# Attention with a gated two-layer network: ones taken out of the value tiles, softmax sums of the global queries made apart, their normalisation put a pair later, and the first batches' work reordered

## The chip, the cores and the metric

The kernel runs on one core of a Trainium2 chip. The metric is the time of one execution on the device in microseconds (us), lower is better. A run of a kernel is several such executions with other kernels in between on the same chip; where a kernel was timed in rounds, every round also ran the kernel before, so that ratios compare the same chip and the same minutes. In the profiles PE is TensorE (the matrix engine), DVE is VectorE, ACT is ScalarE, POOL is GpSimd and SP issues the DMA transfers. PSUM is the memory that TensorE writes its results to. The granted clock is the share of TensorE's full clock that the profile records; here a record is either full or half.

## The reference

Eight batches of eight heads with 512 local positions and 32 global positions of 64 numbers each. A local position attends to the 32 global keys and to local keys within 32 positions. A global query attends to all 544 keys. The 4352 rows that come out go through a network of two matrices with a gate.

```python
s_g = scale * q_g @ concat(k_g, k_l).T            # global queries: 32 x 544
out_g = softmax(s_g) @ concat(v_g, v_l)
s_ll = where(|i - j| <= 32, scale * q_l @ k_l.T, -1e9)
out_l = softmax(concat(scale * q_l @ k_g.T, s_ll)) @ concat(v_g, v_l)
x = concat(out_g, out_l)                          # per batch 544 rows of 8*64 = 512
h = x @ w_in                                      # 512 -> 2048
out = (h * clip(h + 3, 0, 6) / 6) @ w_out         # 2048 -> 512
```

## The kernel before

Work goes by pairs of heads: pair `p` is batch `p // 4`, pair `p % 4` of it (32 pairs). Pairs 0 to 7 (batches 0 and 1) are the head of the kernel, in which weights and inputs still arrive; from pair 8 on one loop body is repeated. The scheduler of the language orders each engine's queue between the pins that the kernel sets; GpSimd's and the DMA queue's order is pinned in every turn of the loop.

Three parts matter. First, the products of the global queries (`emit_PG`). Each head's value tile is 128 columns wide, 64 values and 64 ones, so the same matmul gives the weighted values in rows 0 to 63 and the softmax's sum in rows 64 to 127. All four pairs of a batch collect in one PSUM tile `pg` of a pool with a single buffer:

```python
def emit_PG(p):                                   # ten matmuls of 128x32 a pair
    if m == 0:
        pgs[b] = psg.tile([P, NM, 2, Sg], FP32, tag="pg", name="pg")   # psg: bufs=1
    for e in range(2):
        for u in range(NT):
            nc.tensor.matmul(out=pg[:, m, e], lhsT=vt[:, u, h], rhs=Eg[:, u, e], ...)
        nc.tensor.matmul(out=pg[:, m, e], lhsT=vgs[b % NV][:, h], rhs=Eg[:, NT, e], ...)
```

Second, the normalisation `emit_XG(b)`, which reads `pg` and so sets it free. The logarithm and exponential on ScalarE make the reciprocal, VectorE multiplies:

```python
def emit_XG(b):
    for e in range(2):
        nc.scalar.activation(out=Lg[e * D:(e + 1) * D], in_=pg[D:P, :, e], func=LN)
    nc.scalar.activation(out=Rg, in_=Lg, func=EXP, scale=-1.0)
    for e in range(2):
        nc.vector.tensor_tensor(out=xg[r, :, b], in0=Rg[r], in1=pg[0:D, :, e], op=mult)
```

Third, the loop. `M(n)` puts in n units of the network (four matmuls of 128x512 each, psH for the first matrix, po for the second), which is TensorE's filler:

```python
for p in range(2 * NM, NPAIR):
    feed(p)                       # loads of pair p+5, casts of pair p+4, transposes of pair p+3
    M(n[0]); emit_S2(p + 1)       # local scores, exp on ScalarE, mask multiply on VectorE
    M(n[1]); emit_SG(p + 1)       # global scores, exp on ScalarE
    M(n[2]); emit_AV(p); emit_PG(p)
    M(n[3]); emit_X(p)            # transposes of the normalised rows by DMA into xt
    if m == NM - 1:
        emit_XG(b)                # right after the batch's last products
        units += moe_units(...)
    pin(*QUEUES)
```

The softmax here doesn't subtract the row's maximum and nothing guards it: scores larger than these inputs give would overflow.

## Time and profile before

| kernel before | |
|---|---|
| median of 3 runs (lowest to highest) | 330.34 us (329.37 to 331.39) |
| span of the profiled execution, mean granted clock | 327.7 us, 0.993 |
| TensorE busy | 308.8 us, 94% |
| last w_out cast done | 55.6 us |
| first local scores of batch 2 | 75.03 us |

The table gives times after the span's start. The busy strips, TensorE's waits and GpSimd's timeline stand in the prediction. Three lines are added here, because the result turns on them. The first is the point where the loop proper begins, in TensorE's timeline of the kernel before (start, length, engine, line, operation, result and inputs, shape, count):

```profile
75.03 0.62 PE L258 MATMUL psS<-qT,kT 64*128 64x128 f16 x16
```

The second and third are the groups, by shape, of ScalarE's and VectorE's part in `emit_XG` (total busy us, then mean ns of one, then idle time of the engine in front of them):

```profile
L374 ACT ACTIVATE Lg<-pg 64x128 f32<-64x128 f32 x16 | 4.4, 274 | 3.1 <-PE pg L349 2.2
L378 DVE TENSOR_TENSOR xg<-Rg,pg 64x128 f16<-64x128 f32 x16 | 4.5, 280 | 2.5 <-ACT Rg L375 2.4
```

Per batch that is two logarithms, one exponential and two multiplies, each about 0.3 us: some 1.4 us in a row, started as soon as the batch's last products are there.

### The profile page before, as it was taken

How to read it: one execution, taken by the hardware profiler on the slowest of the kernel's cores; microseconds unless marked ns; L12 is line 12 of the kernel's file. 1: busy time of each engine (PE TensorE's matmuls, PEld its weight loads, DVE VectorE, ACT ScalarE, POOL GpSimd, SP SyncE). 2: the span in 40 equal slices, each digit the busy share in tenths (PEclk: the TensorE clock that was granted, in tenths of full speed). 3: DMA queues.
4: the chain of work that ended last, by engine and by line, in shares of the span. 5: the costliest groups of instructions: out<-in, count | busy, mean ns of one | idle time of the engine just before them, and what ended most of it. 6: DMA issues, size and time to landing. Idle time of an engine off the chain costs nothing.

```text
span 327.7 us, 7442 instructions
## 1 busy us (share of the span) xinstructions
PE 308.8 (94%) x2792; PEld 162.5 (50%) x2792; DVE 219.0 (67%) x482; ACT 196.2 (60%) x388; POOL 133.6 (41%) x226
## 2 busy tenths in 40 slices
PE   7698798979899889999999999999999999999996
PEld 3453354544455445555555555554555555448444
DVE  6677876677666759747985787579755883379201
ACT  3676673878534359546864686468655971379200
POOL 7986899165563363345544642255130000000000
PEclk9799999999999999999999999999999999999999
DMA  7999998299999999999999968898954003100122
GB/s 198 309 375 253 307 341 194 62 194 200 182 180 236 210 189 200 166 204 200 184 154 204 226 124 148 189 214 146 146 130 112 4 16 98 64 0 2 32 90 72
DMA packets 142979, 53.70 MB, mean 164 GB/s; under 512 B 130272, under 2 KB 134624, under 8 KB 142944
## 3 DMA queue, kind: packets, MB, share of 16 engines
q1 hardware_dynamic: 140768, 52.97, 75.3%
q0 software_dynamic: 2176, 0.26, 2.6%
q8 instruction: 22, 0.36, 0.5%
q14 instruction: 13, 0.11, 0.1%
HBM read 35.13 MB, written 8.91 MB: 134 GB/s over the span
## 4 chain that ended last, share of the span: by engine, by line
PE 70%; DMA 12%; DVE 6%; SPq 5%; ACT 3%; POOL 3%; issue 1%; POOLq 0%; ACTq 0%
PE po L406 31%; PE psH L390 27%; DMA qT<-qn 4%; DMA stg<-in_moe_w_in_dram 4%; PE psS L258 3%; DMA stg<-in_v_l_dram 3%; DVE gt L397 2%; ACT t L395 2%; SPq L120 2%; PE pav L324 2%; PE pav L327 2%; PE pg L347 1%; PE po L418 1%; SPq L123 1%; DVE E L265 1%
## 5 line engine op out<-in xcount | busy, mean ns | idle before, releaser
L406 PE MATMUL po<-wout,gt 128*128 128x512 f16 x528 | 121.2, 379 | 0.0
L390 PE MATMUL psH<-xt,win 128*128 128x512 f16 x512 | 119.2, 379 | 1.9 <-DMA xt<-xn 1.0
L397 DVE SCALAR_TENSOR_TENSOR gt<-t,psH 128x512 f16<-128x512 f32 (+1 forms) x144 | 91.0, 653 | 29.1 <-ACT t L395 28.5
L395 ACT ACTIVATE t<-psH,half_col 128x512 f32<-128x512 f32 (+1 forms) x144 | 91.8, 669 | 26.5 <-PE psH L390 25.8
L390 PEld LDWEIGHTS <-win 128*128 128x128 f16 x576 | 53.1, 98 | 52.9 <-issue 2.2
L406 PEld LDWEIGHTS <-gt 128*128 128x128 f16 x528 | 48.5, 98 | 53.5
L262 ACT ACTIVATE E<-psS 128x512 f16<-128x512 f32 x96 | 49.6, 604 | 39.2 <-PE psS L258 39.2
L265 DVE TENSOR_TENSOR E<-E,mk 128x512 f16<-128x512 f16 x96 | 52.0, 574 | 12.7 <-ACT E L262 11.3
L246 POOL COPY qT<-qT 128x32 f16<-128x32 f16 x24 | 5.5, 230 | 97.8 <-DMA qT<-qn 97.7
L410 ACT COPY ot<-po 128x512 f32<-128x512 f32 x16 | 9.4, 586 | 39.4 <-PE po L406 39.4
L410 DVE COPY ot<-po 128x512 f32<-128x512 f32 x17 | 11.7, 691 | 31.5 <-PE po L406 31.4
L333 DVE TENSOR_TENSOR xn<-pav,rc 128x256 f16<-128x256 f32 x64 | 26.2, 421 | 1.5
L136 POOL CAST vt<-stg 128x512 f16<-128x512 f32 x32 | 21.1, 660 | 1.2 <-DMA stg<-in_v_l_dram 1.1
L141 POOL COPY vb<-vt 64x512 f16<-64x512 f16 x32 | 20.7, 646 | 2.1
L332 DVE RECIPROCAL rc<-pav 128x4 f32<-128x4 f32 x64 | 10.3, 172 | 16.0 <-PE pav L327 15.9
L136 POOL CAST kn<-stg 128x512 f16<-128x512 f32 x31 | 19.3, 622 | 3.4 <-DMA stg<-in_k_l_dram 2.6
L136 POOL CAST qn<-stg 128x512 f16<-128x512 f32 x31 | 20.2, 650 | 0.9 <-PE psTk L222 0.5
L324 PE MATMUL pav<-vt,E 128*128 128x65 f16 x256 | 20.3, 194 | 0.0
L327 PE MATMUL pav<-vb,E 128*128 128x65 f16 x256 | 20.3, 195 | 0.0
L287 ACT ACTIVATE E<-psS 128x512 f16<-128x512 f32 x32 | 17.4, 594 | 4.8 <-PE psS L283 4.3
L324 PEld LDWEIGHTS <-E 128*128 128x128 f16 x256 | 18.0, 98 | 3.7 <-issue 0.2
L327 PEld LDWEIGHTS <-E 128*128 128x128 f16 x256 | 17.1, 98 | 3.0
(85 smaller groups left out, 266.0 us busy)
## 6 DMA issues: line engine op xcount, KB each, us to landing
stg<-in_k_l_dram SPq DMA_DIRECT2D x32, 256.0 KB, 3.5
stg<-in_q_l_dram SPq DMA_DIRECT2D x32, 256.0 KB, 4.1
stg<-in_v_l_dram SPq DMA_DIRECT2D x32, 256.0 KB, 5.0
out_dram<-ot SPq DMA_DIRECT2D x23, 256.0 KB, 2.5
stg<-in_moe_w_in_dram SPq DMA_DIRECT2D x16, 256.0 KB, 6.4
stg<-in_moe_w_out_dram SPq DMA_DIRECT2D x16, 256.0 KB, 5.2
out_dram<-ot SPq DMA_DIRECT2D x8, 192.0 KB, 2.4
out_dram<-ot SPq DMA_DIRECT2D x16, 64.0 KB, 1.9
```

What stands on the lines that cost most here:

```text
L136: eng.tensor_copy(out=o, in_=s[c + "f"])
L141: eng.tensor_copy(out=vbs[b % NV][0:D, :, hs, 0:D], in_=vts[b % NV][D:P, :, hs, 0:D])
L262: nc.scalar.activation(out=E[:, ch, e], in_=pss[2 * ch + e], func=EXP, scale=qk_scale)
L265: nc.vector.tensor_tensor(out=E[:, ch, e], in0=E[:, ch, e], in1=mk[:, ch].rearrange("p w c -> p (w c)"), op=mult)
L324: nc.tensor.matmul(out=o, lhsT=E[:, 0, e, w * P:(w + 1) * P], rhs=vt[:, w, h, 0:D + 1], start=True, stop=False, skip_group_check=True)
L327: nc.tensor.matmul(out=o, lhsT=E[:, 1, e, w * P:(w + 1) * P], rhs=vb[:, (w - 1) % NT, h, 0:D + 1], start=False, stop=True, skip_group_chec ...
L333: nc.vector.tensor_tensor(out=xn[:, 2 * w2:2 * w2 + 2].rearrange("p w (e d) -> p w e d", e=2), in0=pv[:, :, :, 0:D], in1=rc.to_broadcast([ ...
L390: nc.tensor.matmul(out=ps[:, 0:n], lhsT=w_in_t[m][:, c * P:(c + 1) * P], rhs=rhs(m), start=(m == 0), stop=(m == NM - 1), skip_group_check= ...
L395: nc.scalar.activation(out=t1[:, 0:n], in_=ps[:, 0:n], func=RELU, bias=half_col, scale=1.0 / 6.0)
L397: nc.vector.scalar_tensor_tensor(out=gts[c][:, 0:n], in0=t1[:, 0:n], scalar=1.0, in1=ps[:, 0:n], op0=amin, op1=mult)
L406: nc.tensor.matmul(out=po[t][:, 0:dm], lhsT=gts[c][:, t * P:(t + 1) * P], rhs=w_out_t[c // 4][:, c % 4], start=(c == 0), stop=(c == NC - 1))
L410: (nc.scalar.copy if t % 2 else nc.vector.tensor_copy)(out=ot, in_=po[t][:, 0:dm])
```

## The change

Its intent is to shorten TensorE's work in the loop and to fill the gaps of the head. The value tiles of two heads now lie side by side with a one at each end, so that one matmul of 128x64 serves both heads of a pair. The softmax's sums no longer come from ones in the value tile: GpSimd adds the five pieces of the exponentials (`sum_E`), and one matmul with a 128x128 tile of ones per batch (`emit_den`) sums over partitions. A reciprocal on VectorE replaces the logarithm and exponential. In the loop, `emit_den` and `emit_XG` of a batch come one pair later than before, after the local scores of the next batch's second pair. In the head, pair 2's keys and queries are loaded ahead of all values, keys and queries of batch 2 are loaded and cast in the middle of w_out, and the global scores of batch 0 move into batch 1's attention.

```diff
     def emit_PG(p):
-        for e in range(2):
-            h = 2 * m + e
-            for u in range(NT):
-                nc.tensor.matmul(out=pg[:, m, e], lhsT=vt[:, u, h], rhs=Eg[:, u, e], ...)
-            nc.tensor.matmul(out=pg[:, m, e], lhsT=vgs[b % NV][:, h], rhs=Eg[:, NT, e], ...)
+        for u in range(NT):
+            nc.tensor.matmul(out=o, lhsT=vt[:, u, m, vc], rhs=Eg[:, u] (both heads), ...)
+        nc.tensor.matmul(out=o, lhsT=vgs[b % NV][:, hs] (both heads), rhs=Eg[:, NT] (both heads), ...)
+    def sum_E(p):                                 # called at the end of emit_SG(p)
+        nc.gpsimd.tensor_tensor(out=s2, in0=Eg[:, 0:2], in1=Eg[:, 2:4], op=add)
+        nc.gpsimd.tensor_tensor(out=s2[:, 0], in0=s2[:, 0], in1=s2[:, 1], op=add)
+        nc.gpsimd.tensor_tensor(out=Ess[b][:, m], in0=s2[:, 0], in1=Eg[:, NT], op=add)
+    def emit_den(b):
+        nc.tensor.matmul(out=pgs[b][:, 1] (all pairs), lhsT=ones, rhs=Ess[b] (all pairs), ...)
     def emit_XG(b):
-        for e in range(2):
-            nc.scalar.activation(out=Lg[e * D:(e + 1) * D], in_=pg[D:P, :, e], func=LN)
-        nc.scalar.activation(out=Rg, in_=Lg, func=EXP, scale=-1.0)
         for e in range(2):
             r = slice(e * D, (e + 1) * D)
-            nc.vector.tensor_tensor(out=xg[r, :, b], in0=Rg[r], in1=pg[0:D, :, e], op=mult)
+            nc.vector.reciprocal(out=Rg[r], in_=pg[r, 1, :, e])
+            nc.vector.tensor_tensor(out=xg[r, :, b], in0=Rg[r], in1=pg[r, 0, :, e], op=mult)
     # loads, and likewise GpSimd's casts
-    for i in range(NC):
+    for i in range(8):
         load_w("out", i)
-    load(2 * NM)
+    load(2 * NM, "kq")
+    for i in range(8, NC):
+        load_w("out", i)
+    load(2 * NM, "v")
     # the head of batch 1 and 2 (cut)
+    held = [units.pop(0), units.pop(0)]           # two units kept for later
     ...
     for p in range(NM):
         emit_PG(p)
+    M(2)
+    emit_den(0)
     emit_XG(0)
     # the loop
             emit_S2(p + 1)
+        if m == 0 and b > NRUN:
+            emit_den(b - 1)
+            emit_XG(b - 1)
         M(n[1])
         ...
         if m == NM - 1:
-            emit_XG(b)
             units += moe_units(...)
```

The code is shortened: "(both heads)" and "(all pairs)" stand for index expressions. Cut: the new layout of the value tiles in the local products, the reordering of the first eight pairs' loads, casts and scores, and more warm-up matmuls.

## The prediction

> **What bounds the kernel now.** I read the page first, then the waits of TensorE up to 130 us, the stretches by engine, and the timelines of TensorE, GpSimd and the DMA queue. The page's first two parts:
>
> ```profile
> PE 308.8 (94%) x2792; PEld 162.5 (50%) x2792; DVE 219.0 (67%) x482; ACT 196.2 (60%) x388; POOL 133.6 (41%) x226
> ...
> PE   7698798979899889999999999999999999999996
> PEclk9799999999999999999999999999999999999999
> DMA  7999998299999999999999968898954003100122
> ```
>
> From slice 15 on (123 us) TensorE is full: the stretch 123 to 327.7 us has 201.3 us of it busy, and what is missing is mostly the last eviction and store. So the second part of the kernel pays only for fewer or shorter matmuls. What can be won besides lies in the first 120 us, where several slices show 6 to 8 tenths. One slice has a clock of 0.7 (the stretch 8.2 to 16.4 us: mean 0.79), and slice 7 has DMA at 0.2. Who keeps TensorE waiting there:
>
> ```profile
> PE psS L258 <- POOL qT L246: 3.1, 3, 1.5
> PE psTk L222 <- POOL kn L136: 2.4, 2, 1.5
> PE pg L347 <- DVE vt L501: 2.2, 4, 1.2
> PE psX L363 <- DVE xn L333: 1.3, 4, 0.6
> PE psTq L222 <- POOL qn L136: 1.1, 2, 0.7
> PE psH L390 <- DMA xt<-xn: 1.0, 1, 1.0
> ```
>
> (The columns: us in total, times, longest.) In time these fall as follows. The casts of pair 2 come late at 12.4 us (1.47 us idle, and the clock record halves the clock there for 3.4 us). The casts of batch 1 come late at 31 to 35 us (2.0 us). The memset of ones into the second value tile holds the global products at 69.8 us (2.2 us). The transposed queries of batch 2 come late at 80.5, 87 and 109 us (3.1 us). The reason for the last is in the queue of GpSimd:
>
> ```profile
> 46.43 9.20 POOL L170 CAST wout<-stg 128x512 f16<-128x512 f32 x16
> 55.69 1.89 POOL L144 COPY vb<-vg 32x2048 f16<-32x2048 f16 x1
> 64.61 0.61 POOL L148 COPY vgs<-vg 32x512 f16<-32x512 f16 x1 [7.03 <-PE pg L349]
> 65.28 0.61 POOL L136 CAST kn<-stg 128x512 f16<-128x512 f32 x1
> ...
> 74.44 0.21 POOL L246 COPY qT<-qT 128x32 f16<-128x32 f16 x1 [3.39 <-DMA qT<-qn]
> ```
>
> GpSimd casts w_out until 55.6 us and then stands for 7.0 us behind one small copy that waits for the global products of batch 0. Only then come the casts of batch 2, and the DMA queue issues the first transpose at 68.75 us. DMA idles from about 56 to 63 us, is full from 65 to 110 us, and TensorE runs after it. The scores of the first pair of batch 2 (L258) begin at 75.03 us.
>
> **What the Trainium skill says.** "TensorE: Matmul & The Clock Gate", part 1 (the clock gate): the clock is halved after an idle window of about 3.4 us and restored after a busy one. The trace agrees in size (3.41 us at half clock from 12.4 us) but there the idle was 1.47 us and shorter gaps before it, so a partly idle window was enough. The same page, "Wait — 56ns, not 53.3ns?": matmuls never start closer than about 25 ns however narrow. The trace agrees: ten global matmuls of 128x32 run from 132.43 to 132.69 us, 26 ns each. "GPSIMD Engine Reference", 3.1: an add of two tensors costs about 2.6 cycles an element at the engine's 1.2 GHz (section 1), so 2.17 ns. No run here shows it yet; one-input copies take 0.21 us for 32 elements and 0.61 for 512, that is 0.83 ns an element and 0.18 us fixed. "VectorE: DVE Perf Modes", "First, the fixed hardware budget": a reciprocal is an iterated divide with a repeat count of 8; the trace has it only on 4 elements (172 ns), which tells little.
>
> **The change, part by part.**
>
> Global products. Per pair, ten 128x32 matmuls (0.26 us) become five of 128x64. The nearest row is the global scores, five of 128x64 starting at 138.52 with the next work at 138.67: 30 ns each, so 0.15 us. Saved: 0.11 us a pair. The denominators become one 128x256 matmul with ones a batch; 64 of that width take 296.48 to 303.46 us, 0.109 each. In the 24 pairs and 6 batches of the loop: 24 x 0.11 - 6 x 0.109 = **2.0 us** off TensorE, where TensorE is the bound.
>
> ScalarE loses 6.9 us of logarithm and exponential (16 x 0.274 + 8 x 0.309) and 2.1 us of ones; VectorE loses 1.9 us of ones and gets 16 reciprocals of 64x128. At one element a cycle these cost about as much as the multiply beside them (0.28 us), at eight some 1.2 us, an estimate. Neither engine is the bound in the loop. The 2.2 us wait for the ones goes.
>
> GpSimd gets three adds a pair, one of 128 elements and two of 64. By the skill's figure: (0.28 + 0.18) + 2 x (0.14 + 0.18) = 1.1 us, and with two hand-overs of about 0.06 us (a value cast ends at 32.50, its shift begins at 32.56) **1.2 us a pair**. In the loop (8.4 us a pair, GpSimd a quarter busy) that is hidden. In the head it is not; see below.
>
> Order at the start. Pair 2's keys and queries are loaded and cast ahead of the values, and idle matmuls fill the gaps: I expect the 1.47 us and most of the 1.7 us lost to the half clock to go, and the local part of batch 1 to end at about 51 us in place of 55. But this gain isn't on the path that sets the end, because of what follows.
>
> The head of batch 2. The instruction order of the changed kernel puts GpSimd's sums for pairs 0 to 3 behind the last w_out cast, and both denominator matmuls wait for GpSimd. In GpSimd's order after that cast, at about 55.7 us (before 55.6: two casts of batch 2 are now ahead of it, some memsets are smaller, and its load comes two tiles later): four sums 4.8; the copies of batch 2's global values, a cast and a shift 3.9 (1.89 + 0.6 + 0.6 + 0.6 and gaps); two sums 2.4; casts of pair 9 and the global keys 3.0; two sums 2.4. That ends at 72.2 us, when TensorE may run the second denominator. Three blocks of four psH matmuls (0.87 each, 2.6) stand between it and the first scores of batch 2: 74.8, beside 75.0 before. So by my sum TensorE waits about 3.5 us at the first denominator (it would be there at 57) and 4.5 us at the second (7.3 us of work lies between), and **the time won earlier is spent there**. One psH block fewer has been done by then: 0.9 us lost.
>
> After that point the change pays. The first transposes are issued in front of pair 9's loads, at about 55 us in place of 68.75, the loads of pairs 9 and 10 fill DMA's idle time, and the transposes of pairs 10 and 11 come some 6 to 9 us sooner than before. The idle times of TensorE after 75 us (0.32, 1.36, 1.47, 1.01 and 0.18 in its timeline, **4.3 us**) should go.
>
> Sum: 0.0 (start of batch 2) + 0.9 - 4.3 - 2.0 = -5.4 us, and +0.8 for a clock halved in one of the two long waits (1.7 us at even odds): -4.6, so 325.7 from 330.34.
>
> **The rivals.** (1) GpSimd's adds run at the one-input rate: 0.18 + 0.11 and twice 0.18 + 0.05, 0.75 us and 0.1 of hand-overs. Eight sums then take 2.8 us less, both waits shrink to 2 to 3 us, the clock stays up: -8.2, 322.1. For it: the inputs are fp16 and small. Against: the skill's figure is for this very operation. (2) The denominators hold nothing, since w_out is cast earlier and TensorE arrives later than I think: then the 4 us of the head are kept too and it is near 318. Against: the w_out loads end near 54 us by DMA's rate of 0.85 us a tile, whatever the order. (3) The waits are longer (a load of pair 9 late, the clock halved twice), or the reciprocals are slow enough that the next batch's global products wait for the single PSUM tile, 1 to 2 us a batch for five batches: near 330. For it: that tile has one buffer and its reader now comes a pair later. Against: about 4 us of TensorE work lies between.
>
> **Range and chances.** I hold the sum (325.7) and the first rival (322.1) about equally likely, which gives 323.9, and take a little off for the second: 323.5 us. Eight in ten: 317.5 to 329. Two per cent faster means below 323.7, so it is nearly even: faster 0.52, same 0.46, slower 0.02.
>
> **What would show it.** The group of the adds: 1.1 us of three instructions is my sum, 0.75 the first rival. Waits of psum tile pg on GpSimd of 3 to 5 us each at about 60 and 70 us, none if rival 2 holds. The first scores of batch 2 at 73 to 75 us. No wait of psS on qT after 80 us. Five 128x64 matmuls in 0.15 us. The clock 1.0 in the second slice. I am wrong if the loop itself (from batch 3 on) is more than 2 us shorter or any longer than before, or if the first scores of batch 2 begin before 71 us.

## The result, and the profile after

| | before | after |
|---|---|---|
| median (lowest to highest), 4 runs each | 329.88 us (329.37 to 331.39) | 341.50 us (338.79 to 342.02) |
| profiled span, mean clock | 327.7 us, 0.993 | 340.1 us, 0.974 |
| last w_out cast done | 55.6 us | 59.65 us |
| first local scores of batch 2 | 75.03 us | 78.84 us |

All runs on record here count as fast: none is over 1.5% above the fastest of its kernel. The ratio after to before is 1.0328 (95% interval 1.0261 to 1.0395): 3.3% slower. Here and below a ratio is the mean time of one kernel's fast runs over that of the other's fast runs of the same rounds, so it is not quite the ratio of the medians. The results of the new kernel are correct, as are those of all experiments.

The page of the changed kernel, in the rows that answer to those in the prediction (a slice is 8.5 us here, counted from 0):

```profile
PE 312.1 (92%) x2653; PEld 163.1 (48%) x2653; DVE 226.8 (67%) x496; ACT 187.6 (55%) x360; POOL 166.0 (49%) x322
...
PE   7897999489999799979999699979999999999996
PEclk9998999689999999999999699999999999999999
DMA  7999999949999999988789598898745201300122
```

TensorE is busy for longer with 139 instructions fewer, which is a first sign of a lower clock. The second slice's clock is up, as hoped. But the clock drops in slice 3 (25 to 34 us), in slices 7 and 8 (60 to 77 us) and again in slice 22 (187 to 196 us), a place where the kernel before was full. TensorE's waits of the changed kernel, the longest first (us in total, times, longest):

```profile
PE pg L360 <- DVE xg L393: 9.3, 5, 2.9
PE pg L367 <- POOL Es L348: 6.4, 2, 4.8
PE psGT L197 <- DVE kgn L187: 2.3, 1, 2.3
...
PE psH L405 <- DMA xt<-xn: 0.8, 1, 0.8
```

The waits of psS and psTk no longer lead. The third line is the wait of the global keys' transposes for VectorE's cast of the keys, the fourth that of the network for the first transposed rows (`xt`). The second line is the wait on GpSimd's sums that the prediction has. The first line is new: five times the next batch's first global products (L360) wait for VectorE's multiply (L393) that sets the single `pg` tile free. In TensorE's timeline of the changed kernel:

```profile
64.40 0.37 PE L367 MATMUL pg<-Es,ones 128*128 128x256 f16 x1 [4.79 <-POOL Es L348]
76.05 0.27 PE L367 MATMUL pg<-Es,ones 128*128 128x256 f16 x1 [1.60 <-POOL Es L348]
78.84 0.62 PE L258 MATMUL psS<-qT,kT 64*128 64x128 f16 x16
...
190.12 0.40 PE L360 MATMUL pg<-Eg,vt 128*128 128x64 f16 x4 [2.92 <-DVE xg L393]
```

The five waits are 1.17 (116 us), 2.74 (153 us), 2.92 (190 us), 1.83 (228 us) and 0.63 us (263 us), once a batch. What VectorE does ahead of 190 us is in its own timeline:

```profile
183.33 1.53 DVE L265 TENSOR_TENSOR E<-E,mk 128x512 f16<-128x512 f16 x1 [3.61 <-ACT E L262]
184.78 0.94 DVE L392 RECIPROCAL Rg<-pg 64x128 f32<-64x128 f32 x1
185.65 2.20 DVE L265 TENSOR_TENSOR E<-E,mk 128x512 f16<-128x512 f16 x3
187.77 0.27 DVE L393 TENSOR_TENSOR xg<-Rg,pg 64x128 f16<-64x128 f32 x1
188.06 0.96 DVE L392 RECIPROCAL Rg<-pg 64x128 f32<-64x128 f32 x1
189.05 0.69 DVE L425 COPY ot<-po 128x512 f32<-128x512 f32 x1
189.77 0.29 DVE L393 TENSOR_TENSOR xg<-Rg,pg 64x128 f16<-64x128 f32 x1
```

The normalisation stands in the queue behind a mask multiply of the next pair (L265), which itself waited 3.61 us for ScalarE's exponential; three more of these and an eviction (L425) are mixed in. From the first reciprocal to the last multiply it takes 5.3 us (184.78 to 190.06). TensorE stands from about 187.2 us on. The groups by shape give the sizes:

```profile
L346 POOL TENSOR_TENSOR s<-Eg 128x128 f32<-128x128 f16 x32 | 13.9, 435 | 51.5 <-ACT Eg L302 50.8
L347 POOL TENSOR_TENSOR s<-s 128x64 f32<-128x64 f32 x32 | 10.5, 327 | 2.5
L348 POOL TENSOR_TENSOR Es<-s,Eg 128x64 f16<-128x64 f32 x32 | 10.0, 313 | 2.5
L392 DVE RECIPROCAL Rg<-pg 64x128 f32<-64x128 f32 x16 | 15.2, 952 | 4.4 <-PE pg L367 4.2
```

A reciprocal of 64x128 takes 952 ns, where the multiply of the same shape beside it takes 0.28 us.

In the head, GpSimd's timeline of the changed kernel shows the end of the w_out casts and the first sum behind it:

```profile
57.02 2.67 POOL L170 CAST wout<-stg 128x512 f16<-128x512 f32 x4 [1.40 <-DMA stg<-in_moe_w_out_dram]
59.66 0.42 POOL L346 TENSOR_TENSOR s<-Eg 128x128 f32<-128x128 f16 x1
```

The last part is the clock. Its records have half clock for 3.41 us from 32.2 us, 6.83 us from 62.9 us and 6.83 us from 189.2 us, 17.07 us before the last store; at half speed that is at most 8.5 us of TensorE's work, against one record of 3.41 us before (1.7 us). It does not all reach the end. In the head GpSimd's row of sums sets when the second denominator can run (76.05 us), whatever TensorE's clock: between the two denominators TensorE took 10.05 us (64.40 to 74.45) where the prediction has 7.3, and only waited less for it (1.60 us). In the loop it counts: the pair's turn around 190 us is 14.44 us long (scores at 182.27 and 196.71), an undisturbed one 8.35; 2.92 of the 6.1 us are the wait, which leaves some 3.2 for the clock.

**Where the 12.4 us of the spans come from.** The first scores of batch 2 are 3.8 us later (78.84 - 75.03). One unit fewer is done by then: +0.9. The idle time that the kernel before had after that point is gone: -4.3. The new idle time after 78.84 us is +10.8 (the five waits on VectorE 9.3, the transposes of xt 0.76, one exponential 0.71). Half clock in the loop: +3.2. The shorter global products: -2.0. The sum is +12.4; as the terms are rounded and estimated, agreement to a tenth is luck.

### The profile page after: what moved, and what is told of

Its sections match the earlier page's. It is cut to its first block, busy times and chain, and to the rows that moved or that the text cites. A ratio compares the mean times of both kernels' runs of the same rounds, so it can differ in the third digit from the quotient of the medians.

```text
span 340.1 us, 7296 instructions
## 1 busy us (share of the span) xinstructions
PE 312.1 (92%) x2653; PEld 163.1 (48%) x2653; DVE 226.8 (67%) x496; ACT 187.6 (55%) x360; POOL 166.0 (49%) x322
## 4 chain that ended last, share of the span: by engine, by line
PE 62%; DMA 14%; DVE 8%; POOL 7%; SPq 4%; issue 1%; ACT 1%; POOLq 0%; ACTq 0%
PE psH L405 28%; PE po L421 25%; DMA stg<-in_moe_w_in_dram 4%; DMA stg<-in_v_l_dram 4%; PE psS L258 3%; DVE Rg L392 3%; DVE E L265 3%; DMA stg<-in_moe_w_out_dram 2%; DMA stg<-in_k_l_dram 2%; DMA stg<-in_q_l_dram 2%; SPq L120 2%; PE pav L329 1%; PE pav L326 1%; POOL vt L136 1%; POOL vb L140 1%
## 5 line engine op out<-in xcount | busy, mean ns | idle before, releaser
L405 PE MATMUL psH<-xt,win 128*128 128x512 f16 x512 | 123.6, 388 | 2.0 <-DMA xt<-xn 0.8
L421 PE MATMUL po<-wout,gt 128*128 128x512 f16 x528 | 124.2, 384 | 0.0
L405 PEld LDWEIGHTS <-win 128*128 128x128 f16 x576 | 54.0, 99 | 57.8 <-issue 8.4
L421 PEld LDWEIGHTS <-gt 128*128 128x128 f16 x528 | 49.5, 99 | 53.9 <-issue 2.1
L265 DVE TENSOR_TENSOR E<-E,mk 128x512 f16<-128x512 f16 x96 | 50.6, 555 | 26.1 <-ACT E L262 24.6
L425 ACT COPY ot<-po 128x512 f32<-128x512 f32 x16 | 9.4, 588 | 62.4 <-PE po L421 57.9
L346 POOL TENSOR_TENSOR s<-Eg 128x128 f32<-128x128 f16 x32 | 13.9, 435 | 51.5 <-ACT Eg L302 50.8
L425 DVE COPY ot<-po 128x512 f32<-128x512 f32 x17 | 11.7, 689 | 22.8 <-PE po L421 19.1
L334 DVE TENSOR_TENSOR xn<-pav,rc 128x256 f16<-128x256 f32 x64 | 25.5, 420 | 1.2
L326 PEld LDWEIGHTS <-E 128*128 128x128 f16 x256 | 17.8, 99 | 3.5
L302 ACT ACTIVATE Eg<-psSG 128x256 f16<-128x256 f32 x32 | 12.9, 404 | 10.6 <-PE psSG L301 10.5
```

Of the source, the lines that this page charges most:

```text
L265: nc.vector.tensor_tensor(out=E[:, ch, e], in0=E[:, ch, e], in1=mk[:, ch].rearrange("p w c -> p (w c)"), op=mult)
L326: nc.tensor.matmul(out=o, lhsT=E[:, 0, e, w * P:(w + 1) * P], rhs=vt[:, w, m, c], start=True, stop=False, skip_group_check=True)
L334: nc.vector.tensor_tensor(out=xn[:, 2 * w2:2 * w2 + 2].rearrange("p w (e d) -> p w e d", e=2), in0=po[:, :, 1:1 + P].rearrange("p w (e d) ...
L405: nc.tensor.matmul(out=ps[:, 0:n], lhsT=w_in_t[m][:, c * P:(c + 1) * P], rhs=rhs(m), start=(m == 0), stop=(m == NM - 1), skip_group_check= ...
L421: nc.tensor.matmul(out=po[t][:, 0:dm], lhsT=gts[c][:, t * P:(t + 1) * P], rhs=w_out_t[c // 4][:, c % 4], start=(c == 0), stop=(c == NC - 1))
L425: (nc.scalar.copy if t % 2 else nc.vector.tensor_copy)(out=ot, in_=po[t][:, 0:dm])
```

## The experiments

Three theories were set against each other. **A**: the slow reciprocal and its late place on VectorE hold the single `pg` tile, and this is the larger loss; the clock's drop at 189 us follows from it. **A'** puts the weight on the tile being single: with a second one, the slow reciprocal does no harm. **F**: the head is late because the w_out casts end late, for which the two casts and loads of batch 2 in their midst are to blame. The rival to A was that the head (GpSimd's sums and the clock there) carries the loss, and the loop's waits would only change their name. Where a recorded expectation uses these letters, they are these; its other letters are explained where they stand. The runs came in three lots, each on another chip and with its own runs of the kernel before: 329.55, 329.28 and 329.38 us median.

### e1_log_exp: the reciprocal by logarithm and exponential again, place unchanged

```diff
-            nc.vector.reciprocal(out=Rg[r], in_=pg[r, 1, :, e])
+            nc.scalar.activation(out=Lg[r], in_=pg[r, 1, :, e], func=LN)
+        nc.scalar.activation(out=Rg, in_=Lg, func=EXP, scale=-1.0)
```

> The changed kernel with one edit: the global outputs are normalised as before the change, by logarithm and exponential on ScalarE, in place of the reciprocal on VectorE (16 of 0.95 us); the place in the program stays, between the scores of the next batch's second pair and its first global product. Theory A (the reciprocals are slow, and they stand in VectorE's queue between the denominators and the next batch's first global product, which reuses the same PSUM tile): the waits of pg on xg (9.3 us in five) fall to under 3 us and the clock stays at 1.0 in the loop: about 331 to 333 us, 9 to 10 faster than the changed kernel's 341.5. Rival B (the place alone is at fault, any work there would be late): the waits stay above 6 us and the time above 337.

Measured: 332.36 us, 1.0073 (1.0046 to 1.0099). That is 9.1 us of the loss taken back by one operation. TensorE's waits in this run (the line numbers are shifted by one to five):

```profile
PE pg L368 <- POOL Es L349: 4.2, 1, 4.2
PE psH L410 <- DMA xt<-xn: 2.6, 1, 2.6
...
PE pg L361 <- DVE xg L398: 0.7, 1, 0.7
```

The waits of pg on VectorE fall from 9.3 to 0.7 us, and the drop of the clock at 189 us is gone. A holds for the time of the operation, though this edit moves the work to ScalarE's queue as well as making it shorter. The wait for the first transposes of xt grows from 0.76 to 2.6 us: a loop that arrives sooner meets the transfer, and 3.41 us at half clock follow at 118.9 us. In this run the w_out casts ended at 56.1 us and the second denominator ran at 72.52, close to the predicted 55.7 and 72.2, but the clock was at half for 6.83 us from 71.1 us on, so the first scores still came only at 77.94 us.

### e2_early_norm: reciprocal kept, denominator and normalisation at the end of the batch's last pair

```diff
-        if m == 0 and b > NRUN:
-            emit_den(b - 1)
-            emit_XG(b - 1)
...
         if m == NM - 1:
+            emit_den(b)
+            emit_XG(b)
             units += moe_units(...)
```

> The changed kernel with one edit: in the loop the denominators and the reciprocals are issued at the end of a batch's last pair, as before the change, not a pair later. Theory A (the reciprocals hurt only because the next global product waits for them): no wait of pg on xg, no halved clock after 90 us; 341.5 - 9.3 (idle) - 3.4 (6.8 us of half clock) = 328.8 us. Rival C (16 slow reciprocals cost VectorE 15 us, and this is felt wherever they stand): still above 335.

Measured: 331.03 us over 20 runs, 1.0035 (1.0012 to 1.0058); 328.8 was expected.

```profile
PE pg L367 <- POOL Es L348: 6.3, 2, 4.4
PE psH L405 <- DMA xt<-xn: 2.6, 1, 2.6
```

No wait of pg on VectorE is left, though each reciprocal is as slow as ever. So the loss in the loop needs both: a slow reciprocal and a late place. Either repair takes some 9 to 10.5 us back. The expectation was missed by 2.2 us. In the profiled run (331.74 us) the wait on xt is longer (2.61 in place of 0.76) and 3.41 us of half clock follow it, together up to 3.6 us. The 20 runs show the clock's share: the five with a mean clock of 0.990 took 328.72 to 330.10 us, the three with 0.974 took 332.32 to 332.87 us.

### e8_two_pg: two `pg` tiles, nothing else (the other PSUM pool loses one of seven)

```diff
-    psp = tc.tile_pool(name="psp", bufs=7, space=PSUM)
-    psg = tc.tile_pool(name="psg", bufs=1, space=PSUM)
+    psp = tc.tile_pool(name="psp", bufs=6, space=PSUM)
+    psg = tc.tile_pool(name="psg", bufs=2, space=PSUM)
```

> The changed kernel with one edit: the tile of the global products gets a second PSUM buffer, and the shared pool of banks one less (6 in place of 7). The reciprocals stay slow and late. Theory A' (the loss in the loop is the wait for the single tile, nothing else): no waits of pg on xg and no half clock in the loop, 341.5 - 12.7 = 329 us, if six banks are enough. Rival C (the reciprocals on VectorE delay the other work of the pair): the time stays above 336 with the idle time at other places (pav, psH, psS waiting on VectorE).

Measured: 332.55 us, 1.0091 (1.0064 to 1.0118). The waits of pg on VectorE are gone with the reciprocals slow and late:

```profile
PE pg L367 <- POOL Es L348: 4.9, 2, 4.2
```

So the single tile is the third condition of the loss. The time is not 329 as expected. The head gains nothing: its sums end sooner, but 6.83 us at half clock from 71.7 us on put the first scores at 78.75 us all the same. The wait on xt is 0.76 us longer than in the changed kernel (1.52), and five small waits of 0.16 to 0.30 us in the loop, 1.1 us in all, may be the price of the tile taken from the other pool. The rest of the 3.5 us stays open.

### e3_ones_sum: the sums by matmuls with ones, none on GpSimd

```diff
-        sum_E(p)
...
     def emit_PG(p):
+        for u in range(NT + 1):
+            nc.tensor.matmul(out=pg[:, 1, m] (both heads), lhsT=ones, rhs=Eg[:, u] (both heads), ...)
...
     def emit_den(b):
+        return
```

> The changed kernel with one edit: the sums of the denominators are made on TensorE, five 128x64 products with ones a pair accumulated in PSUM, in place of three adds on GpSimd and one product a batch. Theory D (GpSimd's sums behind the casts of w_out hold TensorE in the head): the waits of 4.8 and 1.6 us at the denominators and the half clock of 6.8 us at 63 to 70 us go, the first scores of batch 2 begin at 70 to 71 us in place of 78.8; against it 24 x 5 x 0.03 = 3.6 us more matmul in the loop, where the waits on xg stay: 341.5 - 8.3 + 3.6 = 336.8. Rival E (the late w_out and the transposes hold the head, the sums are beside it): the first scores stay at 77 us or later and the time rises to 345.

Measured: 326.09 us, 0.9888 (0.9849 to 0.9926): faster than the kernel before by 1.1%, where 336.8 was expected. The head did as expected: no wait on sums, first scores of batch 2 at 70.39 us. The surprise is the loop: the waits of pg on VectorE's multiply are gone as well, though the call of `emit_XG` was not moved. What leads now is 2.5 us on the cast of the global keys, 1.4 us of the scores at 77 us on VectorE's `gt` (new; all runs with the shorter head have it) and 1.2 us on xt. VectorE's timeline says why:

```profile
169.96 0.92 DVE L398 RECIPROCAL Rg<-pg 64x128 f32<-64x128 f32 x1
...
174.25 1.50 DVE L265 TENSOR_TENSOR E<-E,mk 128x512 f16<-128x512 f16 x2 [1.61 <-ACT E L262]
```

With the sums done by TensorE together with the products at 169.5 us, the scheduler put the reciprocals ahead of the next pair's mask multiplies. So this edit removes two things at once, and its time alone does not part them. The next run limits it.

### e7_ones_head: the same for batches 0 and 1 only

```diff
+        if b < NRUN:      # ones matmuls in emit_PG, emit_den returns
...
-        sum_E(p)
+        if b >= NRUN:
+            sum_E(p)
```

> The changed kernel with one edit: for the first two batches alone the denominators are summed on TensorE (five 128x64 products with ones a pair), in the loop they stay with GpSimd and at their late place. Theory D (the chain on GpSimd holds the head: 6.4 us idle and 6.8 us at half clock): first scores of batch 2 at 70 to 71 us, no wait of pg on Es; the waits of pg on xg in the loop stay (about 9 us, clock halved there): 341.5 - 8 = 333 to 334. Rival E (something else, the transposes of pairs 8 to 10, takes the chain's place): the first scores at 75 or later, 338 or more.

Measured: 335.41 us, 1.0196 (1.0158 to 1.0233), 1.4 us above the 333 to 334 expected.

```profile
PE pg L361 <- DVE xg L401: 8.4, 5, 2.7
```

The head is repaired (no wait on sums, first scores at 72.28 us, only 3.41 us of half clock in the whole run, at 34 us), the loop's waits stay. The head is thus worth about 6 us (341.5 - 335.4) and the loop, by e2, about 10; together 16, more than the loss, because the change also has gains.

### e4_wout_first: batch 2's loads and casts behind all of w_out again

```diff
-    for i in range(8):
-        load_w("out", i)
-    load(2 * NM, "kq")
-    for i in range(8, NC):
+    for i in range(NC):
         load_w("out", i)
-    load(2 * NM, "v")
+    load(2 * NM)          # and the same order in the casts
```

> The changed kernel with one edit: the keys and queries of batch 2's first pair are loaded and cast after all of w_out, as before, not between its eighth and ninth tile. Theory F (these two loads, in small packets, put off the end of w_out's casts from 55.7, which I had predicted, to 59.7 us, and with it GpSimd's sums): the casts end at 56 to 57 us, the first denominator waits 1 to 2 us in place of 4.8, first scores of batch 2 at 75 to 76 us: 338 us or a little less. Rival G (the w_out loads are late for another reason, the longer way of all loads before them): the casts still end after 58.5 us and the time is within 1 us of 341.5.

Measured: 338.48, 338.32, 342.36 and 342.60 us; ratio 1.0319 (1.0247 to 1.0391), not to be told from the changed kernel's, where 338 was expected; the two slower runs have a mean clock of 0.979 and 0.974, the other two 0.985. In the profile (of the run of 338.48 us) the w_out casts end at 53.75 us, 5.9 us sooner, and the first denominator no longer waits, but the second does:

```profile
72.53 0.37 PE L367 MATMUL pg<-Es,ones 128*128 128x256 f16 x1 [3.70 <-POOL Es L348]
```

The loop's five waits stay (9.3 us), and the first scores come at 76.59 us, where 75 to 76 were expected. GpSimd's row of work from the first sum of pair 0 to the second denominator takes from 55.83 to 72.42 us, 16.6 us. An earlier end of the casts is in part spent by waiting for what comes next. F may name a cause of the late casts, but a weak one in time. Besides, the end of the casts scatters from profile to profile with the order of loads and casts alike: 55.8 in e7, 56.1 in e1, 56.9 in e8, 58.8 in e2 and 59.7 us in the changed kernel. One profile of e4 cannot part its edit from that scatter.

### e5_early_ones_head: both repairs (e2 and e7)

```diff
+        if b < NRUN:      # in emit_PG and emit_den, as in e7
...
-        if m == 0 and b > NRUN:
-            emit_den(b - 1); emit_XG(b - 1)
         if m == NM - 1:
+            emit_den(b); emit_XG(b)          # as in e2
```

> Both repairs in one kernel: denominators of the first two batches on TensorE, and in the loop the normalisation at the end of a batch's last pair. If the two costs are separate and add up: 331.0 (early normalisation alone) - 8 (head) = 323; by the other sum, 326.1 (ones on TensorE everywhere) - 24 x 5 x 0.03 (3.6 us of products with ones in the loop) = 322.5. If they overlap (the loop takes back what the head wins, through the transposes): 327 or more, no better than ones everywhere.

Measured: 326.70 us, 0.9916 (0.9892 to 0.9940): 0.8% faster than before. Expected were 322.5 to 323. Neither group of new waits is left. The first scores come at 70.61 us. The profile is of the fastest run (323.95 us). But a later wait has grown:

```profile
112.60 2.10 PE L413 MATMUL psH<-xt,win 128*128 128x512 f16 x9 [2.47 <-DMA xt<-xn]
```

The repairs add up to 16.6 us by their own runs (10.5 and 6.1), and 14.8 were got in the median. The profiled run, 17.6 us below the changed kernel, lacks nothing, though the xt wait is in it, 1.7 us longer than in the changed kernel. Its mean clock is 0.995; five of the six slower runs have 0.989 or 0.990. In the profile of e6 (below; 0.989), 3.41 us at half clock follow the xt wait. So a lower clock after that wait is the likelier reason for the missing 1.8 us; no profile of a slower e5 run shows it.

### e6_all: both repairs, and the global keys' load four w_in tiles earlier

```diff
+    load_g(1, 4, "kg")
     for i in range(8, 12):
         load_w("in", i)
-    load_g(1, 4, "kg")
```

> Both repairs, and the global keys of batches 1 to 3 loaded four w_in tiles earlier. In all runs of the changed kernel TensorE waits 2.3 us for their cast at about 30 us and the clock is halved for 3.4 us right after. If that gap is on the path that sets the end (the head being TensorE's own now): 2.3 + 1.7 = up to 4 us less than with both repairs, 319. If the head is held by loads and casts at its end: the same time as both repairs within 1 us.

Measured: 326.97 us, 0.9915 (0.9886 to 0.9944): nothing gained over e5, and the 2.3 us wait at 31.8 us stays. (The wait on xt is 2.87 us here, with 3.41 us at half clock from 113.5 us on.) The load was not what it waited for. VectorE's timeline in that run:

```profile
30.48 0.68 DVE L228 COPY qT<-psTq 128x512 f16<-128x512 f16 x1
31.19 0.26 DVE L230 COPY qT<-qT 128x32 f16<-128x32 f16 x1
31.36 0.35 DVE L187 CAST kgn<-stg 128x384 f16<-128x384 f32 x1
```

VectorE has no idle time in front of the cast: it stands behind the copies of two pairs' transposes, a matter of the queue's order.

### e9_kg_cast, e10_hold_two, e11_both: that cast moved ahead; two units kept for the xt wait; both

```diff
     u1(5)
+    cast_G(1, 4, "kg")                    # e9 (with e6's load), ahead of the transposes' copies
     emit_T(4)
     u1(6)
     emit_T(5, True)
-    cast_G(1, 4, "kg")
...
-        n = (1, 1, 1, 2) if p == 2 * NM else (1, 1, 2, 2) if b == 2 else (1, 2, 2, 3)
+        n = (1, 1, 1, 2) if p == 2 * NM else (1, 1, 2, 0) if p == 3 * NM - 1 else ...   # e10
```

> Both repairs, with the global keys' weights loaded four tiles of w_in earlier and their cast put ahead of the fifth tile's transposes' copies in VectorE's queue. Theory: the wait of 2.3 us on that cast at 31.5 us goes, and with it the half clock of 3.41 us that followed it (1.7 us): with e5's 326.7 us that makes about 323. Rival: the projection that starts sooner only waits on the next thing, or the half clock is put elsewhere, and the time stays within 1 us of e5's 326.7.

> Both repairs, and two units of TensorE work are held back at the end of the third batch of pairs' first part, so that TensorE has something to do while the transposes of the second batch's normalised rows land. Theory: the wait of 2.47 us on that transfer (at 112.6 us in e5) falls to near nothing, and so does the half clock after it where there was one: about 323.5 to 324.5 us. Rival: the held work is missed where it stood before, and the time stays within 1 us of e5's 326.7.

> Both of the above on top of both repairs. Theory: the gains add, about 320 us, 3 per cent below the kernel before. Rival: each only moves the wait, and the time stays at 325 to 327 us.

| on top of both repairs | median (lowest to highest) | ratio to before (95% interval) |
|---|---|---|
| nothing (e5) | 326.70 us (323.95 to 327.08) | 0.9916 (0.9892 to 0.9940) |
| e9_kg_cast | 325.37 us (323.70 to 327.13) | 0.9874 (0.9842 to 0.9905) |
| e10_hold_two | 325.82 us (323.94 to 327.60) | 0.9888 (0.9850 to 0.9926) |
| e11_both | 324.77 us (323.57 to 326.14) | 0.9857 (0.9835 to 0.9878) |

In e9's profile the 2.3 us wait and the half clock are gone (no half clock before the end), and 1.3 us of the 4 shows in the median. The profiled run has a mean clock of 1.0, but the five others have 0.989 to 0.995, so half clocks do come back in them, as the rival had it. The intervals of e5 and e9 overlap, so even that gain is not certain. For e10 the theory fell:

```profile
113.72 0.38 PE L413 MATMUL psH<-xt,win 128*128 128x512 f16 x1 [2.50 <-DMA xt<-xn]
```

The kept units did run, but the transposed rows landed 3.3 us after their issue in place of 2.5, and the wait is as long as before. Why the transfer took longer is open. e11 beats both kernels: 1.4% under the kernel before, its interval clear of 1, though short of the 2% at which the record calls a kernel faster. The hoped-for 320 us was missed: the wait on xt is still 2.5 us there, and 3.41 us at half clock follow it at 111.9 us.

## Why the prediction was wrong

Point by point, by its own steps.

- **GpSimd's adds.** Right: 435 + 327 + 313 ns are 1.08 us against 1.1 predicted; 1.16 us from one pair's start to the next against 1.2. In the loop no denominator waits for them, as predicted, though GpSimd was nearly half busy there before (38.1 of the 82 us from 123 to 205 us) and not a quarter. Rival 1 (0.75 us) is out. The row of work behind the w_out casts was predicted at 16.5 us (55.7 to 72.2) and took 16.4 (59.65 to 76.05).
- **Waits on the sums.** Right in kind: 4.79 and 1.60 us against 3.5 and 4.5, 6.4 against 8 in all. The second is short because TensorE came later, at half clock (above), and not because GpSimd was quicker.
- **The end of the w_out casts.** Mis-sized: "at about 55.7 us" was 59.65 us. With a row of the right length behind it, the first scores of batch 2 came at 78.84 in place of 74.8 us. The step assumed that the two casts of batch 2 in the middle were made good by smaller memsets. The order may be part of it (e4: 53.75 us); scatter is another (55.8 to 59.7 us).
- **After 80 us.** Right in the main, in part by luck. The 4.3 us counted are 3.15 of psS on the transposed queries, which are gone, 1.01 on xt, which is 0.76 now, and 0.18 of another wait; a wait of 0.71 us on an exponential is new. The first transposes were issued at 53.5 us (predicted about 55), but those of the next three pairs at 74.92, 80.12 and 85.81 us, only 0.5 to 0.7 us sooner than before and not 6 to 9: TensorE no longer waits for them because it comes later itself (its second pair of scores begins at 83.86 us, before at 80.54). In e5, with the head repaired, they are 6.7 to 7.6 us sooner, and psS still does not wait.
- **The loop's matmuls.** Right: five of 128x64 take about 0.15 us, and a pair's turn went from 8.45 to 8.345 us where nothing waits.
- **The reciprocal and the single tile.** This is the step that failed, in rival 3. The prediction gave "at one element a cycle these cost about as much as the multiply beside them (0.28 us), at eight some 1.2 us", concluded that "neither engine is the bound in the loop", and put rival 3 aside because "about 4 us of TensorE work lies between". The time was 0.95 us, near the larger estimate. What was left out was the row of work on VectorE: two reciprocals and two multiplies are 2.5 us by themselves, and with three mask multiplies and an eviction mixed in, 5.3 us (the timeline of VectorE above), starting only once ScalarE's exponential had let the first of them go. The cover was as long as predicted (the denominator runs at 182.82 us, TensorE is idle from 187.2), but it was set against the length of one instruction instead of that row, which ended at 190.06 us. e1, e2 and e8 each took on one of the three conditions (slow, late, single), and each left at most 0.7 us of the waits. The rival's size, "1 to 2 us a batch", was nearly right in the mean (9.3 / 5 = 1.9). But five times 1 to 2 us on top of 325.7 are 331 to 336 us, not "near 330", and mostly above the range: the rival was also added up too low. The rest of its cost, some 3.2 us, came through the clock.
- **The clock.** Mis-sized and misplaced: 0.8 us were allowed for it, in the head. There it was halved for 6.83 us and cost nothing at the end, since GpSimd's row decided; in the loop, where none was foreseen, it cost some 3.2 us. The second slice has its full clock as predicted, but a half clock at 32 us, behind the 2.3 us wait for the cast of the global keys, took its place.
- **The numbers.** Predicted 323.5 us (317.5 to 329), measured 341.5. With the loop's waits and the head's sums both repaired (e5) it is 326.7 us. That this lies inside the range confirms little: there batch 2 begins at 70.61 us, 4.4 us sooner than before, a gain that the prediction did not count.

Why a half clock follows some waits of 2.5 us and not others can be read from the traces. Within a run the records of half clock start whole multiples of 3.413 us apart (in the changed kernel those at 32.17, 62.89 and 189.19 us by 9 and 37 times). Cut all 13 profiles into windows on that grid, leaving out the first 8 us and everything from 316 us on, and 1146 windows begin at full clock. The 21 that are followed by half clock have TensorE idle for 1.99 us or more; the other 1125 have at most 1.89. So it matters how much of a wait falls into one window. The wait of 2.74 us at 153 us in the changed kernel lies across a border, with at most 1.89 us of idle time in a window, and costs no clock; that of 2.92 us at 190 us puts 1.99 us into one. Where the borders lie differs from profile to profile. That may be why one kernel's runs scatter with their clock, but runs without a trace cannot show it. (In the start-up, e2 has one drop after a window with 1.71 us.)

What stays open: why the xt transposes landed later in e10, and part of the time of e8.

## What to carry to other kernels

When a reader of a single-buffered tile is moved later or onto another engine, add up its whole row of work in that engine's queue, with what the scheduler puts in between, and set that against the other work until the next writer; one instruction's duration is not the answer. Here a faster operation, an earlier place or a second buffer each removed nearly all of the wait, and each took 9 to 10.5 us back; none was clearly the best. A wait of 2 to 3 us of TensorE can cost its clock besides, by where it happens to fall; a profile of one run does not show how often. And work that a less busy engine takes over is not free in the phase where that engine feeds everything else: here the sums belonged on TensorE in the first two batches.

## What the Trainium skill lacked or had wrong

- "VectorE: DVE Perf Modes", "First, the fixed hardware budget", names the reciprocal's iterated divide with a repeat count of 8 but gives no time for it, and no other page was found that does. Measured: 952 ns for 64x128 in fp32 from PSUM against 282 ns for the multiply of that shape, and about 170 ns for 128x4. Between the two reciprocals that is 6.3 ns an element a partition ((952 - 170) / 124).
- "TensorE: Matmul & The Clock Gate", "HAM oscillation — how this bites in real kernels", gives as the rule that no idle gap should exceed about 3.4 us. Here the clock was halved in or after gaps below it: 2.92 us (6.83 us at half clock, from within the gap on), 2.61 us in e2 (then 3.41 us); while e7 had gaps of 2.66 and 1.8 us in the loop without any drop. What the runs show is a share of a window: 1.99 us or more of idle time in a window of 3.413 us was followed by half clock, 1.89 us or less was not (above). The page's window of about 3.4 us agrees with the records' lengths, 3.41 us and twice that.
- "GPSIMD Engine Reference", 3.1, about 2.6 cycles an element for two inputs: of the right size, but here somewhat less. From 128x64 to 128x128 the add goes from 313 to 435 ns or 327 to 435 ns, that is 1.7 to 1.9 ns an element, beside the 2.17 ns that the page's figure makes; the types differ between the three adds, so this is no exact check.
